# An attention and MLP kernel: denominators of the first four pairs by TensorE, row sums of five pairs partly on GpSimd, a new order of the work

## The chip, the cores and the metric

The kernel runs on one core of a Trainium2 chip. The metric is the device time of the whole program in microseconds; the three runs of the kernel before took 1008.99, 1009.32 and 1010.76 us, with a median of 1009.32 us.

TensorE (PE in the profile) multiplies matrices, VectorE (DVE) does element work and reductions, ScalarE (ACT) activations and copies, GpSimd (POOL) element work between SBUF tiles, SyncE (SP) starts transfers.

## The reference

```python
# attention: q, k, v are (8, 8, 576, 64); omega is (128, 64)
def phi(x):                                   # x is q or k, scaled by 64 ** -0.25
    proj = einsum('bhsd,md->bhsm', x, omega)
    sq = sum(x * x, axis=-1, keepdims=True) / 2.0
    h = proj - sq
    h = h - max(h, axis=-1, keepdims=True)
    return exp(h) / sqrt(m)
q_p, k_p = phi(q_s), phi(k_s)
kv = einsum('bhsm,bhsd->bhmd', k_p, v)
z = sum(k_p, axis=2)
num = einsum('bhsm,bhmd->bhsd', q_p, kv)
den = einsum('bhsm,bhm->bhs', q_p, z) + 1e-06
attn = num / den
# MLP on the 4608 tokens of 512 features, 2048 hidden
h = x @ w_in
out = (h / (1 + exp(-h))) @ w_out
```

The weights arrive in double precision.

## The kernel before

**Tiling.** Attention is cut into 32 pairs: one pair is two heads of one batch, and four pairs (0 to 3) make the first tile of 512 tokens by 512 features. A pair has nine blocks of 128 token rows. For k and for q of each pair the kernel loads the array twice: turned (`raw`, for the projections, L541 and L547) and as it is (`nat`, for the row sums of squares). ACT squares `nat` (`square`, L524), DVE sums its rows (`square_sum`, L533) and takes the maxima of the projections out of PSUM (`top`, L554 and L556); two small reductions (`shift`, L562) make the bias `nb`, and ACT does the exponentials (`expo`, L579).

**Denominator and numerator.** For the first pairs `zsum_direct` (L628, L630) sums k's features over all tokens by multiplying with a block of ones: the result is z, the same in all 128 rows. `denom` (L639) then makes the products of q's features with z and their sums on DVE, ten instructions with an accumulator read behind each, and one reciprocal of 128x9 (L644). `normal` (L669) multiplies q's features by it on GpSimd, three instructions per pair. TensorE turns the normalised features (`turn`, L675), ACT copies them to SBUF (`en_copy`, L685), and `numer` (L711) multiplies them with kv. ACT rounds the result (`x_high`, L730), DVE subtracts to keep the rest (`x_low`, L735); both parts feed the MLP's first product (`stage1`, L886).

**MLP.** For the first three tiles `stage1` and `stage2` (L1132) run over 16 blocks of hidden features. The step for one block needs all four pairs of the tile. Before it, each weight block is put together from double words on DVE (`word`, L809, L811, L815) and split in two on GpSimd (L828, L832). The rest of the tiles go through a scheme with fewer products (L971, L1085), which the change leaves as it is.

**What sets the order.** Every piece of work is a unit with an engine, a cost, a key and its dependences. `Plan.run` lists the units once, on the host, into one order for each engine, by keys that the long string `SHIFTS` moves and by constants such as `STAY` and `JOIN`. On the chip each engine works through its list in order. Where the list leaves TensorE waiting, `pulses` (L500) puts products of a block of ones there, whose results nobody uses.

Of the kernel before, what the change touches and what calls it, by code (L numbers as in the profile page):

```python
# [9 lines left out]
F32 = mybir.dt.float32  # L10
# [4 lines left out]
ALU = mybir.AluOpType  # L15
# [27 lines left out]
LEAD = 4  # L43
WARM = 7
# [10 lines left out]
for _f in range(16):  # L55
# [24 lines left out]
STAY = 5.387  # L80
HANDOFF = {"PE": 0.053, "ACT": 0.034, "DVE": 0.034, "POOL": 0.075, "SP": 0.08}
CALM = 0.341
JOIN = 0.929
WAIT_PE = 0.279
WAIT_ACT = 0.228
WAIT_DVE = 0.243
WAIT_POOL = 0.0
HASTE = 2.036
# [3 lines left out]
EASE = 0.082  # L92
# [11 lines left out]
    "nb": (0.29, 0.37), "ssum": (0.66, 0.745), "den": (3.41, 3.49),  # L104
# [15 lines left out]
    "mkVzphES3T8Pha5xQn+L-UyFew72pi5OPWk0reil7VtnJIflaampwvp00rwVNdu0MlbFQ3mXIpFWXVQqTVWAh2n5lGMadWEFuMErPdltG3I-qz"  # L120
    "Njj8aLV-cUZEz92d39AIqdihAIAIfIA9w9AIA-+20PI88lPhg1dZAyrHN6CW-4JYJLhIAIm2YbHATZSbP1FlHzrMAIxbqCh6AeNPYGeEDRZFsK"
    "V260v0dWO17cdxwGIh6FFERZ7SVN8-6Y+ErCUPAIur-QGICPkQ3mTLqTgNn8yB455fx-u11n3A1DsOJatjjs09nPLXPmgj-4AIC2mdVWPZh82-"
    "xjzpvQAIvTynbmnYgSb8YhfaHoRB4R65pj6NcQmkjEKCYxVofLgLq1btU4iNXeYUbbXSJFJgWWTlLFaBSxmGFLebN1OuZIEtDlEoa0R6i-7i8X"
    "3hOpGSMDyZpXM2Tt2ybo2CJVdtsitDXRPPBkGPTrRwHVFvwHAIXXwOR4F3y+UOXAYYzBCySXA8JyWgRRRcG18vHmCFsmEaF6nJZphVkR6lzX-4"
    "NKBJG-eBVcLHUuEoOBldPSBWtZzb0g7eQKEPHZ6HLceiwdsoG-POE8yii5DsH3AIi4AIAIAIbuJqV+kQAuREAqDOOgAeLKbgknqhwCvE+IQzhg"
    "QOAwZFpr4WUm4Hg0aGD8FNti6bi6VFH2IGqIBHoaVEjfNNOh6+eqbJ1V0x+y-B8x0Tic5hQoMac2zg1AU7ODIYwaZWAIDXXm3hj6mvuUh6spNS"
    "pWcNUNLINoKMH2PyAIoB5TmFKvKzLZLQmZ6HVZ3oEekZAIVReEz17ryW6Mbok-b5LnPNrhg1YcRsjX0UeId1CSAIvxn4vpiAUDFvO0BFAIC+B0"
    "FrFbTvUEECApKUuSksWBUrCHlOJ0FR4dPNUzKgPYPHCfoc44rkr3rYtAP-4rXPDiOMMNLMMSaSAIMTgZEUAuFSNZL8UuSVPVG3AIBSWsE-fjVh"
    "BLA4B+UdAIr-+sR6EaYvI9vtY8APCsFFlNAIdWcsGVG-QnFjLDKYAMAIAISWU-F8kTZHJBCbAoBYZmAMAIASjIwU4xpv21AIAOkWdvQxIWC-r+"
    "mgHBGdytuN-3u2eyDdd5k1zrkcW-DD3qeEc0tElRgu4Gk1zWCyAINfAIs+dc0haFbJAeVF-4JQAI4FpQfP13979ut0A6RbRnZC1Vlye5qjFGf9"  # L130
    "AI8YzTcrjAAILGdf+6VRSKvcidj+knAIfq7erfv62f4uAsnO5ANEbyURoXRHOtRfUiq1BZGGmw9zei4+3L0hzY8diOuwwEcZiMmIB4Dq0ccHqj"
    "ss1b5wwcFV8dnUj2mooJCjAIbQYw42tdhH-4wU7MzYp1e5Z4xVwj6jdf7Wm1lA7l11dICcv7-4zT4D8ju2S3bPd+l7mDVTGqeoiNJq-45K3C7T"
    "FBAIElVBZG4FbZVFmongYIIr5w-48p5M-4-4yyx+AgJok5R47nL1-4AIsb-4efBt9-uV-4m48vvzXGBrNGjykkiQSkeImwQemccx6h-JIBAIDx"
    "BAsjRQPQzqA30by+Dvgrt9-4jsfBgCgUNKGUCow0nsRzn6iX5qO5c81AHeIRy-VPmd-4Cwl2qXuUQigIcVZQ3FabtQAIccGmAIAVqz-47rAITa"
    "bSyXyp3oiNLxWWLfeRp45c5O+L9AnBahluAjNPWhWj92TJ4OCbSElVAIDLYVLEQG4ec0eHnpgjJWD+AJJGZgWgSgF4RLWPD5ZTc1n9jqApAeAI"
    "S5HZAIFLFGFV1JBoWPridVw3w4iddKSCG0HGKQLjd8l6-etrFJ5HBuAI2AvQAIwCDdOEMSlsAIGusDD-KfAuHoE-IKzjJHUZXRLgEjAIGaE6He"
# [54 lines left out]
)  # L191
HOT = 100.0
PULSE = 0.24
IDLE = 0.791
PAD = 0.288
EARLY = 0.9

# [1533 lines left out]
```

## Time and profile before

| what | value |
|---|---|
| median of three runs | 1009.32 us |
| the profiled execution's own time | 1008.95 us |
| its span | 1007.2 us |
| PE busy in the span | 982.9 us (98%) |
| DVE busy | 758.1 us (75%) |
| ACT busy | 637.4 us (63%) |
| POOL busy | 394.2 us (39%) |
| mean granted TensorE clock | 0.995 |

The span is what the profiler saw from first to last instruction; 1.75 us of the execution lie around it. A busy PE counts everything that it multiplies, the fillers of L500 too.

### The profile page before, as it was taken

The page shows a single profiled execution, that of the slowest core. Times are in us where ns is not written, and L with a number is a line of the kernel's source. Part 1 is how long each engine was busy: PE and PEld are TensorE (multiplying, and loading weights), DVE is VectorE, ACT ScalarE, POOL GpSimd, SP SyncE. Part 2 cuts the span into 40 slices and gives each one's busy share as a digit, 9 for nine tenths or more (in the row PEclk, how much of TensorE's full clock was granted, in tenths as well). Part 3 has the DMA queues.
Part 4 walks back from the last instruction along what each step waited for, and adds up shares of the span by engine and source line. Part 5 has one row for each costly group of instructions (what it writes and reads, how often), then busy time and mean ns, then how long its engine had stood idle before and what let it go on. Part 6 is the DMA issues. An engine that isn't in the chain of part 4 may idle for free.

```text
span 1007.2 us, 17418 instructions
## 1 busy us (share of the span) xinstructions
PE 982.9 (98%) x5790; PEld 784.8 (78%) x5790; DVE 758.1 (75%) x1899; ACT 637.4 (63%) x1239; POOL 394.2 (39%) x495
## 2 busy tenths in 40 slices
PE   8789999999999999999999989999999999999998
PEld 7577777777777777778778768777878777888886
DVE  7997988776677767897667799994649987546953
ACT  7778574656557766658988756667678554334541
POOL 1544564677888777654555321330112010000000
PEclk9999999999999999999999999999999999999999
DMA  9757777777777886749788657876545677656682
GB/s 352 284 181 247 257 238 232 243 245 215 262 240 241 273 284 189 265 137 300 270 289 286 213 180 249 270 245 207 167 159 172 203 263 256 194 190 189 188 277 99
DMA packets 107593, 232.94 MB, mean 231 GB/s; under 512 B 14705, under 2 KB 39409, under 8 KB 107505
## 3 DMA queue, kind: packets, MB, share of 16 engines
q1 hardware_dynamic: 107344, 231.58, 70.0%
q8 instruction: 46, 0.75, 0.3%
q14 instruction: 43, 0.34, 0.1%
q10 hardware_dynamic: 160, 0.26, 0.1%
HBM read 182.52 MB, written 49.28 MB: 230 GB/s over the span
## 4 chain that ended last, share of the span: by engine, by line
PE 78%; DVE 15%; ACT 3%; DMA 2%; issue 1%; SPq 0%; DVEq 0%; ACTq 0%
PE ps_acc L971 17%; PE ps_acc L1132 12%; PE ps_acc L1085 11%; PE ps_h L886 7%; PE ps_fx L886 5%; PE ps_att L541 4%; PE ps_att L651 2%; DVE prod L639 2%; PE ps_att L1085 2%; PE ps_att L711 2%; DVE w L1075 2%; PE ps_fx L971 2%; PE ps_att L971 2%; PE ps_h L971 2%; PE ps_h L1085 2%; PE ps_fx L1085 2%
## 5 line engine op out<-in xcount | busy, mean ns | idle before, releaser
L971 PE MATMUL ps_acc<-w,x 128*128 128x512 f32 x768 | 185.8, 395 | 0.3 <-DVE wraw L1018 0.2
L971 PEld LDWEIGHTS ps_acc<-w,x 128*128 128x128 f32 x768 | 141.9, 188 | 32.7 <-DVE wraw L1018 0.8
L669 POOL TENSOR_TENSOR hq<-hq,rd 128x384 f32<-128x384 f32 x96 | 88.6, 947 | 187.8 <-DVE rd L644 144.2
L1132 PE MATMUL ps_acc<-wo,gh 128*128 128x512 f32 x384 | 123.3, 402 | 0.0
L1085 PE MATMUL ps_acc<-w,x 128*128 128x512 f32 x426 | 108.6, 397 | 0.1
L886 PE MATMUL ps_h<-x,w 128*128 128x512 f32 x360 | 97.2, 403 | 0.6 <-ACT gf L1025 0.3
L1085 PEld LDWEIGHTS ps_acc<-w,x 128*128 128x128 f32 x426 | 79.9, 190 | 18.0 <-DVE w L1075 0.6
L1132 PEld LDWEIGHTS ps_acc<-wo,gh 128*128 128x128 f32 x384 | 68.4, 188 | 14.4
L886 PEld LDWEIGHTS ps_h<-x,w 128*128 128x128 f32 x360 | 64.5, 188 | 15.2 <-ACT gf L1025 1.4
L1132 PE MATMUL ps_acc<-wo,gl 128*128 128x512 f32 x192 | 75.4, 393 | 0.4 <-DVE gl L1029 0.4
L1085 PE MATMUL ps_acc<-gh,x 128*128 128x512 f32 x196 | 70.0, 397 | 0.4 <-DVE gf L1105 0.4
L602 POOL TENSOR_TENSOR t<-hk 128x256 f32<-128x256 f32 x48 | 38.2, 816 | 57.5 <-ACT hk L579 31.4
L1029 DVE TENSOR_TENSOR gl<-gf,gh 128x512 fp32r<-128x512 f32 x48 | 44.4, 931 | 17.3 <-ACT gf L1025 17.1
L886 PE MATMUL ps_fx<-x,w 128*128 128x512 f32 x216 | 56.7, 399 | 0.0
L886 PEld LDWEIGHTS ps_fx<-x,w 128*128 128x128 f32 x216 | 39.4, 188 | 10.1 <-issue 1.1
L639 DVE CUSTOM_DVE_ANT_0 prod<-hq,ps_att 128x128 f32<-128x128 f32 (+1 forms) x140 | 40.1, 287 | 8.1 <-PE ps_att L622 2.5
L1085 PEld LDWEIGHTS ps_acc<-gh,x 128*128 128x128 f32 x196 | 36.8, 188 | 9.2 <-DVE gf L1105 0.8
L524 ACT ACTIVATE nat<-nat 128x576 f32<-128x576 f32 x58 | 40.1, 703 | 4.8 <-DMA nat<-qn 2.8
L1132 PEld LDWEIGHTS ps_acc<-wo,gl 128*128 128x128 f32 x192 | 36.0, 188 | 9.0 <-DVE gl L1029 1.0
L685 ACT COPY en<-ps_att 128x384 f32<-128x384 f32 x55 | 25.7, 480 | 22.5 <-PE ps_att L675 18.0
L608 POOL TENSOR_TENSOR t<-t,hk 64x128 f32<-64x128 f32 x48 | 25.0, 520 | 34.6 <-ACT hk L579 31.9
L1085 PE MATMUL ps_acc<-gl,x 128*128 128x512 f32 x98 | 38.3, 391 | 0.0
(464 smaller groups left out, 2461.4 us busy)
## 6 DMA issues: line engine op xcount, KB each, us to landing
x<-ws SPq DMA_DIRECT2D x84, 512.0 KB, 4.2
x<-wt SPq DMA_DIRECT2D x44, 512.0 KB, 4.0
wo<-wo_d SPq DMA_DIRECT2D x32, 512.0 KB, 4.8
x<-wo_d SPq DMA_DIRECT2D x64, 256.0 KB, 3.3
rawk<-kT SPq DMA_DIRECT2D x30, 352.0 KB, 3.9
rawq<-qT SPq DMA_DIRECT2D x30, 352.0 KB, 4.8
v<-v SPq DMA_DIRECT2D x30, 320.0 KB, 4.6
nat<-kn SPq DMA_DIRECT2D x29, 288.0 KB, 4.5
```

The costliest lines, as they stand in the source:

```text
L524: nc.scalar.activation(nat, nat, AF.Square, scale=SCALE * 0.5**0.5)
L541: nc.tensor.matmul(ps[:, i * M : (i + 1) * M], raw[r, o : o + P], oms[r], start=True, stop=True)
L602: nc.gpsimd.tensor_tensor(t[:, step], e[:, 5 * step : 5 * step + 2], e[:, 5 * step + 2 : 5 * step + 4], ALU.add)
L608: nc.gpsimd.tensor_tensor(es[r, j], es[r, j], e[r, MID], ALU.add)
L639: nc.vector.tensor_tensor_reduce(out=prod[r], in0=e[r, c], in1=z[r, j * M : (j + 1) * M], scale=1.0, scalar=GUARD, op0=ALU.mult, op1=ALU.a ...
L669: nc.gpsimd.tensor_tensor(e[:, c], e[:, c], rd[:, c].unsqueeze(2).broadcast_to([P, 3, M]), ALU.mult)
L685: nc.scalar.copy(T["en", n][:, 3 * g * P : 3 * (g + 1) * P], T.pop(("t", n, g)))
L886: nc.tensor.matmul(ph, w[:, i], x[:, j], start=k == 0 and n == 0, stop=k == NK - 1 and n == 2)
L971: nc.tensor.matmul(ph, ws[:, u, kk * P : (kk + 1) * P], o[:, x], start=i in (0, 1, 4) and kk == 0 and n == 0, stop=kk == 1 and n == 2, ski ...
L1029: nc.vector.tensor_tensor(gl, T.pop(("gf", t, f)), T["gh", t, f].bitcast(F32), ALU.subtract)
L1085: nc.tensor.matmul(T["qb", p, chain][d], w[:, u, d * P : (d + 1) * P], x, start=i in (0, 1, 4) and s == 0 and n == 0, stop=s == NS - 1 and ...
L1132: nc.tensor.matmul(T["po", t][j], g[:, js], w, start=f == 0 and n == 0, stop=f == NF - 1 and n == 2)
```

## The change

For pairs 0 to 3 (`n < SHARE`) the sum z is made with a block of ones 64 columns wide, so that it comes out with its 128 features on the partitions, repeated in 64 columns for each head (`zsum_wide`). ACT copies it to SBUF (`z_copy`). q's features are turned without having been normalised, and the numerator's product is followed by the same product with z (`numer_denom`): the denominators stand in 64 rows per head, beside the numerators. ACT copies them out and adds the guard (`den_copy`), DVE inverts them, 128x512 and 128x64, and multiplies them into the numerator (`divide`). `denom` and `normal` are gone for these pairs; `x_high` and `x_low` read the quotient from SBUF.

For pairs 1 to 5 (`TREE`) the squares are made on GpSimd, which then adds the upper half of each row to the lower three times (`fold`: 32, 16, 8 columns). DVE sums the 8 that are left and scales the sums.

`SHIFTS`, and constants of the planner, are new; so the order of the units is new everywhere. The core of the diff:

```diff
+SHARE = 4
+TREE = range(1, 6)
-STAY = 5.387
+STAY = 13.011
-JOIN = 0.929
+JOIN = 2.248
-IDLE = 0.791
-PAD = 0.288
+IDLE = 0.638
+PAD = 0.475
...
     def square(n, who):
         nat = T["nat", n, who]
+        if n in TREE:
+            nc.gpsimd.tensor_tensor(nat, nat, nat, ALU.mult)
+            return
         nc.scalar.activation(nat, nat, AF.Square, scale=SCALE * 0.5**0.5)
...
+        s, nat = sums_at(n, who)[:, 1, :NC], T.pop(("nat", n, who))
+        if n in TREE:
+            nc.vector.tensor_reduce(s, nat[:, :, :8], AX.X, ALU.add, negate=True)
+            nc.vector.tensor_scalar(s, s, SCALE * SCALE * 0.5, None, ALU.mult)
+            return
+        nc.vector.tensor_reduce(s, nat, AX.X, ALU.add, negate=True)
+
+    def fold(n, who, w):
+        nat = T["nat", n, who]
+        nc.gpsimd.tensor_tensor(nat[:, :, :w], nat[:, :, :w], nat[:, :, w : 2 * w], ALU.add)
...
+    def zsum_wide(n, ps):
+        e = T["h", n, "k"]
+        for j in range(2):
+            for i in range(5):
+                c, one = (5 * j + i, ones[:, :D]) if i < 4 else (MID, sides_of[:, j, :D])
+                nc.tensor.matmul(ps[:, j * D : (j + 1) * D], e[:, c], one, start=i == 0, stop=i == 4)
+        T["z", n] = ps
+
+    def z_copy(n):
+        T["zw", n] = zw = new("zw", [P, P])
+        nc.scalar.copy(zw, T.pop(("z", n))[:, :P])
+
+    def numer_denom(n, a, b, c):
+        numer(n, a, b)
+        for ps, lo, hi, at in ((c, 0, MAIN, 0), (b, MAIN, S, P + REST)):
+            for j in range(2):
+                nc.tensor.matmul(
+                    ps[j * D : (j + 1) * D, at : at + hi - lo], T["zw", n][:, j * D : (j + 1) * D],
+                    T["en", n][:, j * S + lo : j * S + hi], start=True, stop=True,
+                )
+        T["dp", n] = [(c, MAIN, 0), (b, REST, P + REST)]
+
+    def den_copy(n):
+        T["dn", n] = new("gl", [P, MAIN]), new("xr", [P, REST])
+        for d, (ps, w, at) in zip(T["dn", n], T["dp", n]):
+            nc.scalar.activation(d, ps[:, at : at + w], AF.Identity, bias=guard)
+
+    def divide(n):
+        T["xf", n], T["xr", n] = new("gf", [P, MAIN]), new("xr", [P, REST])
+        for x, d, (ps, lo, hi, at) in zip((T["xf", n], T["xr", n]), T.pop(("dn", n)), T["num", n]):
+            nc.vector.reciprocal(d, d)
+            nc.vector.tensor_tensor(x, ps[:, at : at + hi - lo], d, ALU.mult)
```

Where it moves instructions, on DVE first: the place behind the exponentials of pair 0. `smk`, `smq` are the sums and maxima, `nbk`, `nbq` the biases, `w_...` in a TENSOR_REDUCE a squared array, `x_391` the first quarter of x. Before:

```order
L639 ISA prod,den<-hq,ps_fx 128x128
L639 ISA den 128x1
L644 RECIPROCAL rd<-den 128x9
L556 TENSOR_REDUCE smq<-ps_acc 128x4 x2
L554 TENSOR_REDUCE smq<-ps_acc 128x1
L562 TENSOR_REDUCE smq<-smq 128x9
L562 TENSOR_REDUCE nbq<-smq 128x9
```

After:

```order
L553 TENSOR_REDUCE smk<-w_194 128x9
L554 TENSOR_SCALAR smk<-smk 128x9
L589 TENSOR_REDUCE smk<-smk 128x9
L589 TENSOR_REDUCE nbk<-smk 128x9
L553 TENSOR_REDUCE smk<-w_199 128x9
L554 TENSOR_SCALAR smk<-smk 128x9
L553 TENSOR_REDUCE smq<-w_197 128x9
L554 TENSOR_SCALAR smq<-smq 128x9
L690 RECIPROCAL gl<-gl 128x512
L691 TENSOR_TENSOR gf<-ps_fx,gl 128x512
L690 RECIPROCAL xr<-xr 128x64
L691 TENSOR_TENSOR xr<-ps_att,xr 128x64
```

The two instructions shown of the 20 rows of `denom` are gone; in their place stand two inversions and two products, and ahead of them three row sums of GpSimd's arrays (194 and 197 of pair 1, 199 of pair 2).

On POOL, from the start of its work. Before, the first rows are pair 0's normalisation and the first weight:

```order
L488 MEMSET sides 64x128 x2
L669 TENSOR_TENSOR hq<-hq,rd 128x384 x3
L828 CAST w_492<-w_468 128x512
L832 TENSOR_TENSOR w_492<-w_468,w_492 128x512
L669 TENSOR_TENSOR hq<-hq,rd 128x384 x3
```

After, three squares and nine halvings come first:

```order
L541 TENSOR_TENSOR w_194<-w_194 128x576
L541 TENSOR_TENSOR w_197<-w_197 128x576
L541 TENSOR_TENSOR w_199<-w_199 128x576
L560 TENSOR_TENSOR w_194<-w_194 128x9x32
L560 TENSOR_TENSOR w_194<-w_194 128x9x16
L560 TENSOR_TENSOR w_194<-w_194 128x9x8
L560 TENSOR_TENSOR w_199<-w_199 128x9x32
L560 TENSOR_TENSOR w_199<-w_199 128x9x16
L560 TENSOR_TENSOR w_199<-w_199 128x9x8
L560 TENSOR_TENSOR w_197<-w_197 128x9x32
L560 TENSOR_TENSOR w_197<-w_197 128x9x16
L560 TENSOR_TENSOR w_197<-w_197 128x9x8
```

Pair 0's and pair 1's normalisations are gone from here, and all ten squares and 30 halvings stand before the third weight's first row.

On PE, the end of pair 0's work. Before, from its turned blocks to its numerator:

```order
L675 MATMUL ps_fx<-ident,hq 128x128 x3
L675 MATMUL ps_acc<-ident,hq 128x128 x3
L675 MATMUL ps_fx<-ident,hq 128x128 x3
L547 MATMUL ps_fx<-oms,w_213 128x128
L711 MATMUL ps_acc<-en,kw 64x512 x2
L711 MATMUL ps_acc<-en,kw 64x64 x2
```

After:

```order
L735 MATMUL ps_acc<-ident,hq 128x128 x3
L719 MATMUL ps_acc<-ident,kt 128x128
L735 MATMUL ps_acc<-ident,hq 128x128 x3
L735 MATMUL ps_fx<-ident,hq 128x128 x3
L771 MATMUL ps_fx<-en,kw 64x512 x2
L771 MATMUL ps_att<-en,kw 64x64 x2
L676 MATMUL ps_att<-en,zw 64x512 x2
L676 MATMUL ps_att<-en,zw 64x64 x2
```

The turns of pair 0 now stand ahead of the other pairs' projections, and the product with z follows the numerator.

## Rows read from the trace of the kernel before

**Rows 1.** The page: busy time by engine; PE in 40 equal slices.

```profile
PE 982.9 (98%) x5790; PEld 784.8 (78%) x5790; DVE 758.1 (75%) x1899; ACT 637.4 (63%) x1239; POOL 394.2 (39%) x495
...
PE   8789999999999999999999989999999999999998
```

**Rows 2.** Stretches: length, busy PE, PEld, DVE, ACT, POOL, clock, DMA share, GB/s.

```profile
0.00:80.00 80.00, 68.32 (x576) 54.99 (x577) 68.01 (x218) 57.85 (x164) 31.07 (x42) 0.96 0.76 270
40.00:50.00 10.00, 7.58 (x69) 5.87 (x65) 9.00 (x37) 7.45 (x26) 4.28 (x5) 0.87 0.80 294
50.00:60.00 10.00, 9.01 (x65) 7.13 (x65) 9.83 (x20) 7.51 (x26) 2.44 (x3) 0.79 0.27 89
80.00:180.00 100.00, 97.62 (x584) 77.10 (x584) 86.95 (x198) 66.51 (x134) 53.53 (x50) 1.00 0.73 246
...
5.73:71.32 65.59, 55.52 (x507) 44.24 (x503) 60.01 (x203) 47.20 (x143) 25.37 (x28) 0.95 0.80 291
```

**Rows 3.** DVE in order of time: start, length, instruction, idle before it.

```profile
5.73 0.75 DVE L533 TENSOR_REDUCE smk<-nat 128x9 f32<-128x576 f32 x1 [4.45 <-ACT nat L524]
...
14.96 0.28 DVE L639 CUSTOM_DVE_ANT_0 prod<-hq,ps_fx 128x128 f32<-128x128 f32 x1
...
18.69 1.23 DVE L556 TENSOR_REDUCE smq<-ps_acc 128x4 f32<-128x512 f32 x2
...
30.14 0.74 DVE L533 TENSOR_REDUCE smq<-w 128x9 f32<-128x576 f32 x1
30.80 0.74 DVE L533 TENSOR_REDUCE smq<-nat 128x9 f32<-128x576 f32 x1
...
60.97 0.28 DVE L639 CUSTOM_DVE_ANT_0 prod<-hq,ps_fx 128x128 f32<-128x128 f32 x1
...
65.03 0.69 DVE L533 TENSOR_REDUCE smq<-nat 128x9 f32<-128x576 f32 x1
...
71.32 0.68 DVE L735 TENSOR_TENSOR x<-ps_att,x 128x512 fp32r<-128x512 f32 x1
```

**Rows 4.** PE in order of time, up to the first second-stage product.

```profile
27.95 2.05 PE L500 MATMUL ps_h<-ones 128*128 128x128 f32 x16 [1.55 <-ACT kw L664]
...
35.54 1.08 PE L711 MATMUL ps_att<-en,kw 128*64 128x512 f32 x4 [1.00 <-ACT en L685]
...
36.66 0.49 PE L547 MATMUL ps_acc<-oms,w 128*128 128x128 f32 x2
36.99 0.39 PE L628 MATMUL ps_acc<-hk,sides 128*128 128x128 f32 x2
...
39.31 1.31 PE L651 MATMUL ps_fx<-hk,w 128*64 128x128 f32 x20
...
80.65 0.62 PE L1132 MATMUL ps_acc<-wo,gh 128*128 128x512 f32 x2
```

**Rows 5.** DVE by group and shape: count, busy us, mean ns, idle before.

```profile
L644 DVE RECIPROCAL rd<-den 128x9 f32<-128x9 f32 x32 | 6.9, 216 | 1.6
...
L554 DVE TENSOR_REDUCE smk<-ps_att 128x1 f32<-128x128 f32 x18 | 5.2, 287 | 7.7 <-ACT en L685 4.4 <-PE ps_att L547 2.0 <-PE ps_att L675 1.2
...
L584 DVE TENSOR_SCALAR hk<-ps_att,nbk 128x128 f32<-128x128 f32 x11 | 3.9, 350 | 0.5 <-ACT en L685 0.2
...
L562 DVE TENSOR_REDUCE smk<-smk 128x9 f32<-128x18 f32 x4 | 0.7, 174 | 0.1
```

**Rows 6.** GpSimd in order of time: pair 0's normalisation.

```profile
18.96 2.40 POOL L669 TENSOR_TENSOR hq<-hq,rd 128x384 f32<-128x384 f32 x3 [17.04 <-DVE rd L644]
```

**Rows 7.** GpSimd's additions on tile t: count, ns least/median/most, first and last start.

```profile
L602 POOL TENSOR_TENSOR t<-hk x48: 722/738/1235, 187.6 to 758.6; 128x256 f32<-128x256 f32 x48
L608 POOL TENSOR_TENSOR t<-t,hk x48: 446/456/1013, 192.5 to 777.9; 64x128 f32<-64x128 f32 x48
```

**Rows 8.** ACT in order of time: squares of pair 1 and 2.

```profile
12.81 1.35 ACT L524 ACTIVATE w<-w 128x576 f32<-128x576 f32 x2
```

**Rows 9.** DVE's first or-step of a weight, 0 to 130 us: least/median/most.

```profile
L811 DVE SCALAR_TENSOR_TENSOR w<-wre,w x20: 680/693/1775, 22.8 to 128.1; 128x512 uint32<-128x512 uint32 x20
```

More of the change, by code (lines that the diff above doesn't have):

```diff
@@ L120 @@
[L120 to L124, printed above, removed]
@@ L1178, in attention_mlp @@
                 order=before, alloc=[(HOMES.get(("nat",) + w, "nat"), ("nat",) + w)], lat=1.1)
[L1179 removed]
+            folded = n in TREE
+            add(("sq",) + w, "POOL" if folded else "ACT", 0.7, at(n, 2 * i - 4, 13 + 10 * i - 32), lambda n=n, who=who: square(n, who),
                 after=[("nat",) + w], alloc=[(f"sm{who}", ("sm",) + w)])
+            for x in (32, 16, 8) if folded else ():
+                add(("fold", n, who, x), "POOL", 0.4, at(n, 2 * i - 4 + 0.02 * (32 - x), 13 + 10 * i - 32), lambda n=n, who=who, x=x: fold(n, who, x),
+                    after=[("sq",) + w if x == 32 else ("fold", n, who, 2 * x)])
             add(("ssum",) + w, "DVE", 0.76, at(n, 2 * i - 3, 14 + 10 * i - 32), lambda n=n, who=who: square_sum(n, who),
[L1182 removed]
+                after=[("fold", n, who, 8) if folded else ("sq",) + w], order=prev("ssum"), free=[("nat",) + w])
             o = 6.2 + 10.8 * i
@@ L1264, in attention_mlp @@
             alloc=[("kw", ("kw", n))], free=[bk(kx)], reads=[bk(kx)])
-        add(("den", n), "DVE", 3.5, at(n, 8, 34.2), lambda n=n: denom(n), after=e["q"] + [zn],
-            order=[("den", n - 1)] if n else [], alloc=[("den", ("den", n)), ("rd", ("rd", n))], free=[bk(zn)], reads=[bk(zn)])
-        plan.freed_by[("den", n)] = [("den", n)]
+        shared = n < SHARE
+        if shared:
+            add(("zc", n), "ACT", 0.3, at(n, 6.9, 0), lambda n=n: z_copy(n), after=[zn], alloc=[("zw", ("zw", n))], free=[bk(zn)])
+        else:
+            add(("den", n), "DVE", 3.5, at(n, 8, 34.2), lambda n=n: denom(n), after=e["q"] + [zn],
+                order=[("den", n - 1)] if n > SHARE else [], alloc=[("den", ("den", n)), ("rd", ("rd", n))], free=[bk(zn)], reads=[bk(zn)])
+            plan.freed_by[("den", n)] = [("den", n)]
         for g in range(3):
-            add(("norm", n, g), "POOL", 0.85, at(n, 9 + 0.1 * g, 37 + 0.1 * g), lambda n=n, g=g: normal(n, g),
-                after=[("den", n)], order=[("norm", n, g - 1)] if g else [], free=[("rd", n)])
+            if not shared:
+                add(("norm", n, g), "POOL", 0.85, at(n, 9 + 0.1 * g, 37 + 0.1 * g), lambda n=n, g=g: normal(n, g),
+                    after=[("den", n)], order=[("norm", n, g - 1)] if g else [], free=[("rd", n)])
             joint = DIRECT <= n < NWIN - 1
@@ L1294, in attention_mlp @@
         homes_of = [(f"x{k}{t % 2}", ("x", t, k))] if t < PLAIN else []
-        add(nm, "PE", dur, at(n, 10, 60.5), lambda a, b, n=n, f=kv_numer if follow else numer: f(n, a, b),
-            after=after, alloc=homes_of, free=free, banks=2)
+        if shared:
+            add(nm, "PE", 2.2, at(n, 10, 60.5), lambda a, b, c, n=n: numer_denom(n, a, b, c), after=after + [("zc", n)], alloc=homes_of,
+                free=free + [("zw", n)], banks=3)
+            add(("dn", n), "ACT", 0.8, at(n, 10.1, 0), lambda n=n: den_copy(n), after=[nm], alloc=[("gl", ("dn", n)), ("xr", ("dr", n))], free=[bk(nm, 2)])
+            add(("dv", n), "DVE", 0.9, at(n, 10.15, 0), lambda n=n: divide(n), after=[("dn", n)], alloc=[("gf", ("xf", n)), ("xr", ("xr", n))],
+                free=[bk(nm, 0), bk(nm, 1), ("dn", n), ("dr", n)])
+        else:
+            add(nm, "PE", dur, at(n, 10, 60.5), lambda a, b, n=n, f=kv_numer if follow else numer: f(n, a, b),
+                after=after, alloc=homes_of, free=free, banks=2)
         p, j = divmod(t - PLAIN, 2)
```

201 lines of the change are left out of this document (111 added, 90 removed), and 2 rows, old and new, of the table RINGS.

## Prediction

> **What bounds the kernel now.** First the page: PE is busy for 982.9 of 1007.2 us, and its slices are full but for the first three, the one with an 8 near 600 us and the last [rows 1]. So outside the start time is only won by taking work from PE, and the change takes none there. [...] Part of the busy time is filler: 16 rows for eight products take 2.05 us, so the 16 products in the order cost 16 x 0.26 = 4.2 us [rows 4]. **The start thus holds 11.7 + 2.9 + 4.2 = 18.8 us that are no work**; from 80 to 180 us it is 2.4 us [rows 2].
>
> Who makes PE wait there? DVE. From its first row sum at 5.73 us to the subtraction that finishes the first tile's x, at 71.32, it works through its list almost without a gap: 60.0 of 65.6 us are busy, and what is missing is the few hundredths between one short instruction and the next [rows 2, 3]. PE has 55.5 busy us in the same stretch, ACT 47.2, POOL 25.4. Behind that subtraction lie the products for three hidden blocks, and the first second-stage product starts at 80.65 [rows 4]. From then on PE is saturated. So the change is to be priced by what it does to DVE's list up to the fourth subtraction; PE's own work is a second floor.
>
> **DVE's list.** Removed: four denominators. The first occupies DVE from 14.96 to 18.69, the fourth from 60.97 to 65.03 [rows 3]: 3.73 and 4.06 us, four at 3.9 are 15.6. (Pair 4's denominator stands ahead of the fourth subtraction before and after.) The ten row sums of pairs 1 to 5 cost 0.66 from start to start [rows 3]; the new one reduces 72 elements, near the 0.17 of the row with 18 inputs, and a scaling that waits for it [rows 5]; I take 0.35. Ten save 3.1.
>
> Added, four times: an inversion and a product of 512 columns, and both of 64. The products are like the two maxima that take 1.23 together [rows 3]: 0.6, and 0.15 for the small one. The inversion of 512 is not in the trace; the nearest row is the one of nine elements at 0.216 us [rows 5]. A reduction of 18 inputs to 9 takes 0.174, so 0.042 us are in excess. If that is a fixed charge, 512 elements stream like everything else, in 0.6 us. If it belongs to the elements, each costs (0.042 + 0.009)/9 = 5.7 ns more than in a streaming pass, and the two inversions 3.5 + 0.5 = 4.0 us instead of 0.75. A row speaks for the fixed charge: an element-wise instruction on 128 elements takes 0.350 where a reduction over as many takes 0.287 [rows 5], an excess of 0.063 that cannot depend on nine elements. I take 0.75, so 1.5 us for a pair, 6.0 for four; the upper end, 4.75 a pair, is a rival below.
>
> In sum DVE's list gets 15.6 + 3.1 - 6.0 = **12.7 us shorter**. Two things take some of it back.
>
> **GpSimd.** It loses 4 x 2.40 us of normalising [rows 6] and gets ten squares and 30 halvings. By the normalisation (384 elements in 0.80) a square of 576 costs 1.2 and the three halvings, 504 elements, 1.05; by the additions on t (256 elements in 0.738, 128 in 0.456, so 0.17 + 2.2 ns an element) 1.44 and 1.63 [rows 6, 7]. One array thus costs 2.25 to 3.1 us, ten cost 22 to 31. POOL was busy for 25 of DVE's 65.6 us [rows 2], so there is room; the order is what hurts. Ahead of pair 0's first inversion DVE waits for three arrays, whose twelve GpSimd instructions take 6.8 to 9.2 us and can begin when the arrays are in, about 11.5 (ACT has all three squared from 12.81 on [rows 8]). They end between 18 and 21. DVE's own work up to there, two row sums, six maxima of 0.6 and small ones, is some 7.5 us from 5.73, so it stands idle for 5 to 7 us; I take 5.5. Queued behind that wait are pair 0's inversion and the maxima of pair 1's q. Pair 0's own chain would not be much sooner: exponentials, turns, copies, products and one copy end at about 18 too.
>
> [...] The or-step that reads two SBUF tiles has a least time of 0.68 and a worst of 1.775 [rows 9], and some 16 steps with two SBUF inputs stand in the new list up to there (the weights' or-steps, x's subtractions); with GpSimd half as busy again I put 2 us more on them. [...]
>
> So the fourth subtraction comes at 71.32 - 12.7 + 5.5 + 2 = 66.1, 5.2 us earlier, and the first second-stage product, 9.3 us behind it as before, at 75.4.
>
> **PE's floor.** Ahead of that product both orders hold the same 12 projections, 45 turned blocks and 36 first-stage products; after has, in addition, pair 4's kv and numerator (1.3 + 1.1 us [rows 4]), which need not be done later: 2.4 us. The four new products with z cost as much as the numerator, 35.54 to 36.66 [rows 4]: 4 x 1.1 = 4.5. The sum z took 2.3 us (36.99 to 39.31); with half the columns it lies between that and the 1.31 of kv; I take 1.7, which saves 2.4 in four. Nineteen fillers stand in the new order, 4.9 us. Work before was 80.65 - 18.8 = 61.9; now 61.9 + 2.4 + 4.5 - 2.4 + 4.9 = 71.3. That leaves 4.1 us of idle up to 75.4: DVE still sets the end, with PE close behind.
>
> **The sum.** 5.2 us earlier plus 2.4 us done ahead are 7.6. Against that: at the first second-stage product the new DVE list has seven weights put together where the old had eight to nine, and each weight costs DVE two or-steps of 0.69 [rows 9] and a shift, in a stretch where it is busy for 87 of 100 us [rows 2]. I put 1.2 us more idle there. Past 180 us the number of changes between kinds of product on PE is the same in both orders (153), so I take nothing. **6.4 us off the profiled 1008.95 is 1002.5; off the median 1009.32, which lies 0.4 above it, it is 1002.9.** ACT loses ten squares and gains four copies of 0.6, four small ones: it had 18 us of air in the stretch and hides both. The SP queue has the same loads in another order; the fourth pair's arrays are in well before they are needed.
>
> **Rivals.**
>
> *The inversion costs by the element.* Place: the first row of `divide` on DVE, four times, with the maxima of the next pairs queued behind it. At 4.0 us instead of 0.75 the four pairs cost 13 us more on the list that sets the end, and 1002.9 becomes 1016; with some of it in gaps 1013 to 1016. It decides from about 4 ns an element, where the 6.4 us are gone. For it: the excess of 0.042 us in the only row [rows 5]. Against it: the element-wise row with the same excess. [...]
>
> [...]
>
> *The change does what it says, but PE is not waiting for DVE.* Then the 2.1 us of added PE work and three more fillers would show at once: 1012. The idle PE beside the busy DVE [rows 2] speaks against it; I count it with the first rival's chance.
>
> **How the numbers follow.** The forecast, 1002.9, has 0.50 (999 to 1006.5, from 3 to 6.5 us of waits and 1.3 to 2.3 for z); the first rival 0.34 (1009 to 1018, most near 1015); the waits 0.16 (1005.5 to 1009). To hold 8 in 10 the range needs the forecast, the waits and half of the first rival: **999 to 1015**; the forecast's own is 999 to 1006.5. About 0.2%, 2 us, is what a measurement can tell from no change. Faster by more: 0.48 of the forecast, 0.09 of the waits, 0.02 of the rival, 0.59. Within: 0.11. Slower: 0.30, nearly all of it the first rival.
>
> **What would show it.** The inversion of 128x512 at 0.6 to 0.7 us (right) or above 2 (the first rival). The fourth subtraction at 63 to 68 us, the first second-stage product at 73 to 78, with DVE idle for about 5 us before pair 0's inversion, waiting for GpSimd. PE idle in the first 75 us at 4 to 6. From 80 to 180 us idle of 3 to 4, and nothing changed past it. The forecast is wrong if a second stretch appears in which PE waits, or if the new order leaves PE idle past 180 us where its slices are full now.

## The result, and the profile after

The changed kernel takes 1024.24 us (median of 4 runs, 1018.78 to 1026.26), the kernel before 1010.04 beside it: a ratio of 1.0133, 95% interval 1.0091 to 1.0175. Run a second time it gave 1021.56 and a ratio of 1.0119 [1.0092, 1.0145]. It is 1.2 to 1.3% slower, and 6.6 to 9.2 us above the upper end of the predicted range. The profiled execution is its fastest: 1018.78 us with a span of 1017.0, against 1008.95 and 1007.2 before.

The page (busy time; PE in slices; granted clock) and the stretches, the answers to [rows 1, 2]:

```profile
PE 992.3 (98%) x5828; PEld 794.8 (78%) x5828; DVE 764.1 (75%) x1842; ACT 631.8 (62%) x1233; POOL 412.6 (41%) x523
...
PE   8898999999999999999999999999999999999998
...
PEclk9898999999999999999999999999999999999999
```

```profile
0.00:80.00 80.00, 68.43 (x567) 55.74 (x567) 62.13 (x141) 47.99 (x150) 43.64 (x63) 0.91 0.65 224
20.00:30.00 10.00, 7.72 (x71) 6.94 (x70) 9.65 (x15) 3.40 (x11) 9.53 (x12) 0.86 1.04 399
30.00:40.00 10.00, 10.00 (x73) 7.95 (x73) 9.20 (x18) 8.82 (x27) 6.93 (x12) 0.80 0.41 121
40.00:50.00 10.00, 5.87 (x48) 5.06 (x49) 9.60 (x22) 5.30 (x19) 5.75 (x7) 0.88 0.48 163
50.00:60.00 10.00, 10.00 (x87) 8.96 (x88) 6.40 (x18) 6.42 (x24) 4.45 (x6) 0.78 0.31 93
80.00:90.00 10.00, 7.57 (x49) 6.01 (x51) 8.58 (x17) 5.99 (x11) 2.76 (x4) 0.66 0.89 304
80.00:180.00 100.00, 97.07 (x584) 77.90 (x585) 89.89 (x200) 67.58 (x137) 53.98 (x51) 0.97 0.75 251
...
96.18:1017.00 920.82, 910.12 (x5184) 728.26 (x5182) 687.92 (x1676) 571.94 (x1062) 365.40 (x456) 1.00 0.70 229
```

PE is as busy in the first 80 us as before (68.4 and 68.3), but the granted clock is 0.91 where it was 0.96. The stretch at 40 to 60 us is as before (0.88 and 0.78); new are the one at 20 to 40 us (0.86 and 0.80, before 1.00) and the one at 80 to 90 us (0.66, before 1.00), which runs mostly at half the full clock (0.50 from 82 to 88 us). Behind the first second-stage product (the last row; it starts at 96.18, before at 80.65) 920.8 us are left, before 926.6. So 15.5 us are lost up to there and 5.7 come back behind it: PE is busy there for 910.1 us instead of 913.9, since pair 4's products are done ahead as the prediction said (it had put 2.4), and idle for 10.7 us instead of 12.7. That makes 9.8 us, the difference of the two spans. Of the 15.5 only 2.3 are more idle time of PE (14.0 us up to the product, before 11.7). An estimate by the prediction's own way of reckoning, busy time times the missing share of the clock in the five stretches above, puts 8.6 us on the clock where it had 2.9 (7.58 x 0.13 + 9.01 x 0.21 [rows 2]): 5.7 us more. The rest, some 7.5 us, is work that now stands ahead of that product.

VectorE in order of time, the answer to [rows 3] (start, length, instruction, the idle time before it): pair 0's first short row sum and its division, then the division of the fourth pair and its x subtraction.

```profile
16.49 0.23 DVE L553 TENSOR_REDUCE smk<-w 128x9 f32<-128x72 f32 x1 [3.82 <-POOL w L560]
16.75 0.48 DVE L554 TENSOR_SCALAR smk<-smk 128x9 f32<-128x9 f32 x1
...
20.97 3.34 DVE L690 RECIPROCAL gl<-gl 128x512 f32<-128x512 f32 x1
...
27.01 1.45 DVE L799 TENSOR_TENSOR x<-gf,x 128x512 fp32r<-128x512 f32 x1
...
78.22 3.29 DVE L690 RECIPROCAL gl<-gl 128x512 f32<-128x512 f32 x1
81.62 0.69 DVE L691 TENSOR_TENSOR gf<-ps_att,gl 128x512 f32<-128x512 f32 x1
82.22 0.54 DVE L690 RECIPROCAL xr<-xr 128x64 f32<-128x64 f32 x1
82.86 0.23 DVE L691 TENSOR_TENSOR xr<-ps_att,xr 128x64 f32<-128x64 f32 x1
...
84.24 0.68 DVE L799 TENSOR_TENSOR x<-gf,x 128x512 fp32r<-128x512 f32 x1
```

An inversion of 512 columns takes 3.3 us, nearly five times the product behind it (0.69). The fourth subtraction stands at 84.24 instead of 71.32. The groups over the first 100 us show that no inversion is an exception:

```profile
L690 DVE RECIPROCAL gl<-gl 128x512 f32<-128x512 f32 x4 | 13.3, 3330 | 0.0
...
L690 DVE RECIPROCAL xr<-xr 128x64 f32<-128x64 f32 x4 | 2.2, 544 | 0.0
L554 DVE TENSOR_SCALAR smq<-smq 128x9 f32<-128x9 f32 x5 | 2.2, 430 | 0.2
```

And PE, up to the first second-stage product, waits most for the products behind the inversions (L691; waits by releaser: sum, times, longest):

```profile
PE ps_acc L568 <- DVE gf L691: 3.3, 2, 1.9
PE ps_att L568 <- DVE gf L691: 2.5, 1, 2.5
PE ps_att L574 <- DVE xr L691: 2.3, 1, 2.3
PE ps_att L574 <- ACT hk L606: 2.2, 1, 2.2
```

The projections of the next pairs write the PSUM tiles (`ps_acc`, `ps_att`) that the division's products read: 8.1 us of waits. In the kernel before PE's longest wait for VectorE there is 0.7 us, its first instruction apart. Behind one of these waits the trace shows a loss of its own. PE in order of time, behind the 2.3 us for pair 0's division:

```profile
25.95 0.49 PE L574 MATMUL ps_att<-oms,rawq 128*128 128x128 f32 x2 [2.28 <-DVE xr L691]
26.28 1.00 PE L665 MATMUL ps_fx<-ones,hk 128*128 128x64 f32 x8
...
27.49 1.92 PE L665 MATMUL ps_fx<-ones,hk 128*128 128x64 f32 x8
```

The same eight rows take 1.00 us and, 1.2 us later, 1.92: PE waited 2.28 us, and its granted clock, 1.00 from 26 to 27 us, was 0.50 from 28 to 34.

### The profile page after: what moved, and what is told of

Its sections match the earlier page's. It is cut to its first block, busy times and chain, and to the rows that moved or that the text cites. A ratio compares the mean times of both kernels' runs of the same rounds, so it can differ in the third digit from the quotient of the medians.

```text
span 1017.0 us, 17440 instructions
## 1 busy us (share of the span) xinstructions
PE 992.3 (98%) x5828; PEld 794.8 (78%) x5828; DVE 764.1 (75%) x1842; ACT 631.8 (62%) x1233; POOL 412.6 (41%) x523
## 4 chain that ended last, share of the span: by engine, by line
PE 80%; DVE 13%; issue 1%; ACT 1%; DMA 1%; SPq 0%; DVEq 0%; ACTq 0%
PE ps_acc L1035 18%; PE ps_acc L1149 12%; PE ps_acc L1196 12%; PE ps_h L950 7%; PE ps_fx L950 5%; PE ps_att L568 4%; PE ps_att L1149 3%; DVE omr L699 2%; PE ps_att L1035 2%; PE ps_att L771 2%; PE ps_h L1149 2%; PE ps_att L711 2%; PE ps_h L1035 1%; PE ps_att L735 1%; DVE w L844 1%
## 5 line engine op out<-in xcount | busy, mean ns | idle before, releaser
L1035 PE MATMUL ps_acc<-w,x 128*128 128x512 f32 x810 | 196.3, 396 | 1.3 <-DVE w L844 0.7
L1035 PEld LDWEIGHTS ps_acc<-w,x 128*128 128x128 f32 x810 | 149.5, 188 | 35.6 <-DVE wraw L1082 1.3
L729 POOL TENSOR_TENSOR hq<-hq,rd 128x384 f32<-128x384 f32 x84 | 78.9, 963 | 202.3 <-DVE rd L704 172.8
L1149 PE MATMUL ps_acc<-w,x 128*128 128x512 f32 x426 | 108.0, 395 | 0.4 <-DVE w L1139 0.4
L1149 PEld LDWEIGHTS ps_acc<-w,x 128*128 128x128 f32 x426 | 79.1, 188 | 18.3 <-DVE w L1139 0.9
L950 PE MATMUL ps_h<-x,w 128*128 128x512 f32 x348 | 91.8, 400 | 0.0
L699 DVE CUSTOM_DVE_ANT_0 omr<-hq,ps_att 128x128 f32<-128x128 f32 (+1 forms) x180 | 51.6, 286 | 16.8 <-PE ps_att L649 10.8
L950 PE MATMUL ps_fx<-x,w 128*128 128x512 f32 x228 | 60.0, 402 | 2.5 <-DVE hk L611 2.5
L1093 DVE TENSOR_TENSOR gl<-gf,gh 128x512 fp32r<-128x512 f32 x48 | 41.8, 875 | 18.6 <-ACT gf L1089 18.5
L950 PEld LDWEIGHTS ps_fx<-x,w 128*128 128x128 f32 x228 | 41.9, 190 | 12.0 <-POOL wo L892 2.7
L543 ACT ACTIVATE nat<-nat 128x576 f32<-128x576 f32 x54 | 37.1, 695 | 5.3 <-DMA nat<-kn 2.8
L745 ACT COPY en<-ps_att 128x384 f32<-128x384 f32 x46 | 21.9, 483 | 25.1 <-PE ps_att L735 20.8
```

The source lines that it names most:

```text
L543: nc.scalar.activation(nat, nat, AF.Square, scale=SCALE * 0.5**0.5)
L699: nc.vector.tensor_tensor_reduce(out=prod[r], in0=e[r, c], in1=z[r, j * M : (j + 1) * M], scale=1.0, scalar=GUARD, op0=ALU.mult, op1=ALU.a ...
L729: nc.gpsimd.tensor_tensor(e[:, c], e[:, c], rd[:, c].unsqueeze(2).broadcast_to([P, 3, M]), ALU.mult)
L745: nc.scalar.copy(T["en", n][:, 3 * g * P : 3 * (g + 1) * P], T.pop(("t", n, g)))
L950: nc.tensor.matmul(ph, w[:, i], x[:, j], start=k == 0 and n == 0, stop=k == NK - 1 and n == 2)
L1035: nc.tensor.matmul(ph, ws[:, u, kk * P : (kk + 1) * P], o[:, x], start=i in (0, 1, 4) and kk == 0 and n == 0, stop=kk == 1 and n == 2, ski ...
```

## Experiments

Theory: the inversion's price is the error of the prediction. Rival: the rest of the new order (its waits for GpSimd, PE's fixed order) is slow by itself. Ratios are to the kernel before on the same chip. Unless said otherwise an experiment keeps the changed kernel's order and edits only what is issued.

**The changed kernel again.**

> The changed kernel once more, unaltered. Its profiled execution took 1018.78 us, its three timed ones 1023.1 to 1026.3 at a lower mean granted clock (0.983 beside 0.990). If the profiled one was only lucky, this profile comes at 1023 to 1026 and shows the stretch where a second 5 us of the clock go; I expect that in the first 100 us, where the clock of the first profile was already 0.90. If the two figures belong to how the executions are taken, the profile is again near 1019 and the timed ones near 1024.

1021.56 us (1019.26 to 1024.97), the profiled one again the fastest: 1019.26, clock 0.990. The second reading held in the main: the profile is again near 1019, and the others, 1020.9 to 1025.0, reach up to the 1024 that was expected of them. Both profiles agree within 0.5 us at every point that is used here (the fourth subtraction at 84.24 and 84.49, the first second-stage product at 96.18 and 96.39). Where the other executions lose their 1.7 to 7.5 us no profile of this kernel shows; their clock was 0.982 to 0.988.

**No inversion.**

```
-            nc.vector.reciprocal(d, d)
+            nc.vector.tensor_scalar(d, d, 1.0, None, ALU.mult)
```

> The changed kernel in its own order, with each of the eight inversions replaced by a multiplication of the same tile by 1.0: the numerators are multiplied by the denominators and not divided by them. This is the case that the prediction took as likeliest (an inversion that streams). Theory (the inversion's 3.33 and 0.54 us a pair are the whole error): DVE's list gets 4 x (3.87 - 0.6) = 13 us shorter, the fourth subtraction comes at 68 to 72 instead of 84.2, the first second-stage product at 79 to 83, the profiled time at 1004 to 1008, the median near the forecast of 1002.9 to 1008. Rival (the new order's waits for GpSimd and its fixed order cost as much by themselves): not below 1012.

1010.50 us, ratio 1.0010 [0.9998, 1.0022]: 11.1 us less than the changed kernel in the same comparison. The stand-ins took 0.48 and 0.76 us instead of 3.33 and 0.54:

```profile
L690 DVE TENSOR_SCALAR xr<-xr 128x64 f32<-128x64 f32 x4 | 3.0, 762 | 0.0
...
L690 DVE TENSOR_SCALAR gl<-gl 128x512 f32<-128x512 f32 x4 | 1.9, 479 | 0.0
```

So VectorE's list lost 4 x 2.63 = 10.5 us, and the end came sooner by about as much. That is not a chain of VectorE alone: the fourth subtraction came 8.4 us sooner (75.82 for 84.24), and 2 us more were won behind it, where the clock from 80 to 90 us is 1.00 instead of 0.66. The inversions are worth these 11 us. But the time lies between the two expectations, above the theory's and below the rival's, and 7.6 us are still missing to the forecast of 1002.9. In its trace (VectorE and PE in order of time; this profile's first row sum came 1.5 us later than the changed kernel's, behind a load):

```profile
52.39 0.69 DVE L583 TENSOR_REDUCE smq<-ps_att 128x4 f32<-128x512 f32 x1 [4.01 <-PE ps_att L568]
...
75.82 0.68 DVE L799 TENSOR_TENSOR x<-gf,x 128x512 fp32r<-128x512 f32 x1
```

```profile
42.44 0.80 PE L574 MATMUL ps_att<-oms,w 128*128 128x128 f32 x2 [2.33 <-ACT hk L606]
...
85.79 0.62 PE L1196 MATMUL ps_acc<-wo,gh 128*128 128x512 f32 x2
```

Now PE is late too: it waits 2.33 us for exponentials, runs at a clock of 0.62 from 40 to 50 us, and VectorE waits 4.0 us for a projection. The subtraction is at 75.8 where the forecast had 66.1.

**Two pairs without inversion.** The same edit for n < 2 (stream_01) and for n > 1 (stream_23).

> The changed kernel in its own order, with the inversions of pairs 0 and 1 alone replaced by a multiplication by 1.0 (their numerators are multiplied by the denominators and not divided); pairs 2 and 3 are inverted. All four replaced gave 1010.5, none 1021.6 to 1024.2. If each inversion costs the same at the end (VectorE's list is one chain from the start to the fourth subtraction), this gives 1016 to 1018. If the first two fall into time in which VectorE waits for something else anyway, it gives 1020 to 1023.

> The counterpart: pairs 2 and 3 have the multiplication by 1.0 and are not divided, pairs 0 and 1 are inverted. One chain: 1016 to 1018, as its counterpart. If only the last two stand on the path that sets the end: 1011 to 1013.

1016.84 us, ratio 1.0071 [1.0055, 1.0088], and 1014.81, ratio 1.0048 [1.0032, 1.0064]. The first is as one chain would have it; the second lies between its two expectations. Against the changed kernel's 1.0119 the first two pairs give back 4.8 us and the last two 7.2; all four gave 11.0. The parts add up (12.0 and 11.0, within the intervals), for 5.3 us of VectorE's time each. So the first two inversions don't lie in time that is free anyway. Whether the last two weigh more than the first can't be told: the intervals of 4.8 and 7.2 us overlap.

**The squares and row sums back.** In `square`, `square_sum` and `fold` (the short sum and its scaling in `square_sum` go too):

```
     def square(n, who):
...
-            nc.gpsimd.tensor_tensor(nat, nat, nat, ALU.mult)
-            return
...
     def fold(n, who, w):
-        nc.gpsimd.tensor_tensor(nat[:, :, :w], nat[:, :, :w], nat[:, :, w : 2 * w], ALU.add)
+        pass
```

> The changed kernel in its own order, with the squares of pairs 1 to 5 back on ScalarE at the same places, no halvings, and the full row sums on VectorE; the inversions stay. Theory (the inversion is the error, the halvings are right): DVE gains ten times 0.745 - 0.61 us = 1.4 us of work, and loses the 3.8 us wait for GpSimd ahead of pair 0's inversion in part (ScalarE has the squares by 13 to 14 us); ScalarE gets 7 us more. In sum within 4 us of the changed kernel, 1015 to 1023 profiled. [...]

1024.27 us, ratio 1.0138 [1.0118, 1.0158], as the changed kernel: the squares on GpSimd and the waits for them are not what makes it slow, though the profiled execution, 1025.05, lies 2 us above the theory's range. Its trace shows where the time went that VectorE no longer waits for GpSimd:

```profile
21.71 3.35 DVE L687 RECIPROCAL gl<-gl 128x512 f32<-128x512 f32 x1 [4.56 <-ACT gl L682]
```

Without GpSimd VectorE waits for ScalarE's copy of pair 0's denominators, which stands behind the squares there, and the first inversion begins at 21.71 us instead of 20.97. With GpSimd the copy, behind pair 1's exponentials on ScalarE, ended at 20.70, so pair 0's own chain was about as late as the row sums. The same edit without the inversions:

> The changed kernel in its own order with both edits: no inversion (a multiplication by 1.0 in its place, so the numerators are multiplied by the denominators), and the squares and the full row sums of pairs 1 to 5 back on ScalarE and VectorE. With the squares on GpSimd this was 1010.5, so 8 us of the forecast of 1002.9 are missing without any inversion. If GpSimd's work is where they went (its scalings of 9 elements took up to 0.83 us where free ones take 0.17), this is faster than 1010.5: 1004 to 1008. [...]

1008.97 us, ratio 1.0001 [0.9989, 1.0014], beside 1.0010 with GpSimd's squares: above the 1004 to 1008 of the expectation, and the intervals of the two overlap. **In this order the second part of the change neither gains nor costs anything that can be measured**; by the intervals at most some 2.6 of the missing 7.6 us are GpSimd's.

**The second part alone**, in the order of before: the squares of pairs 1 to 5 and their halvings issued on GpSimd where the squares stood on ScalarE, the short sums on VectorE.

```
+        if n in range(1, 6):
+            nc.gpsimd.tensor_tensor(nat, nat, nat, ALU.mult)
+            for w in (32, 16, 8):
+                nc.gpsimd.tensor_tensor(nat[:, :, :w], nat[:, :, :w], nat[:, :, w : 2 * w], ALU.add)
+            return
```

> The kernel before, in its own order, with the second part alone: the squares of pairs 1 to 5 and their three halvings on GpSimd, issued where the squares stood on ScalarE, and the short row sums on VectorE. The denominators are those of before. Theory (the halvings do what the prediction said: ten row sums save 0.3 us each of VectorE's list; GpSimd's instructions wait behind its normalisations, which stand in its queue in another order than would suit them): between 1005 and 1013, near the kernel before. Rival (VectorE's instructions with two inputs in SBUF and its short scalings are held up by GpSimd's for longer than the row sums save): 1012 to 1020.

1023.30 us, ratio 1.0131 [1.0113, 1.0148]: above both expectations. PE's waits in its first 90 us; the last line is the first one's counterpart in the kernel before:

```profile
PE ps_acc L685 <- POOL hq L679: 6.6, 6, 3.0
PE ps_h L896 <- DVE x L745: 4.9, 2, 3.9
...
PE ps_acc L675 <- POOL hq L669: 3.4, 6, 1.1
```

GpSimd is busy for 52.8 of the first 80 us (31.1 before), and pairs 0 to 3 are still normalised there (hq): PE's turned blocks stand behind the halvings. What the rival names is there as well: the scalings of nine elements take up to 0.96 us (0.17 where they are shortest), and PE waits 4.9 us for VectorE's x subtraction. So in the order of before the second part costs 13 us, with the normalising still on GpSimd; whether an order made for it alone would do better was not tried.

**VectorE's list lighter still.** No inversion and nothing in its place, squares on ScalarE, and the row sums of pairs 1 to 5 over 8 of 64 columns:

```
-            nc.vector.reciprocal(d, d)
...
+        if n in TREE:
+            nat = nat[:, :, :8]
         nc.vector.tensor_reduce(s, nat, AX.X, ALU.add, negate=True)
```

> The changed kernel in its own order with VectorE's list made lighter still: no inversion and nothing in its place (the numerators are multiplied by the denominators), the squares on ScalarE, and the row sums of pairs 1 to 5 taken over 8 of the 64 columns only, without halvings and scalings (the sums are wrong). Against the kernel with squares on ScalarE and a multiplication for each inversion (1009.0) VectorE loses 4 x 1.0 us of multiplications and ten times 0.745 - 0.22 us, 9 us in all. Theory (VectorE's list still sets the end of the start, and the missing 8 us of the forecast are terms of that list that I took too low): 1000 to 1004. Rival (with the inversion gone the start is set by TensorE and by what it waits for, the floor that the prediction put 4 us lower): 1006 to 1010.

1005.27 us, ratio 0.9950 [0.9935, 0.9966]: 5.1 us less (0.9950 to 1.0001) for 4 x 1.26 us of stand-ins and ten times 0.52 us of row sums, 10.3 us of VectorE's list; it lies just above the first expectation, below the second. The two profiles differ by less, 3.6 us of span and 2.6 at the first second-stage product (83.76 and 81.19). The first 80 us, then the stretch from 40 to 50 us in the kernel with the stand-ins (squares on ScalarE) and in this one, and what PE still waits for in the 80 us:

```profile
0.00:80.00 80.00, 72.06 (x640) 57.96 (x641) 52.48 (x146) 62.62 (x180) 17.36 (x26) 0.98 0.77 270
...
40.00:50.00 10.00, 7.67 (x48) 7.03 (x50) 7.33 (x19) 7.95 (x28) 2.01 (x2) 0.68 0.53 176
40.00:50.00 10.00, 7.98 (x88) 7.17 (x88) 7.34 (x21) 9.53 (x34) 2.08 (x3) 1.00 0.59 212
```

```profile
PE ps_att L565 <- ACT hk L603: 1.1, 1, 1.1
PE ps_att L512 <- DVE guard L504: 1.1, 1, 1.1
PE ps_h L516 <- ACT hq L603: 1.1, 1, 1.1
PE ps_acc L715 <- ACT kt L712: 0.9, 1, 0.9
```

VectorE is busy for 52 of 80 us, and but for the first instruction PE's waits of over half a microsecond are all for ScalarE. The first second-stage product starts at 81.19, still not ahead of the 80.65 of before; what this kernel wins over the one before lies behind it (922.3 us instead of 926.6). Part of the gain is the clock's, 1.00 from 40 to 50 us instead of 0.68. And the squares are on ScalarE here, which is busy for 62.6 of 80 us (53.0 with the squares on GpSimd and no inversion), so its waits may be this edit's own. That 81 us are the floor of the new order on PE is therefore not shown, only that PE hardly waits for VectorE any more.

**The inversion on ScalarE**, as the exponential of the negative logarithm.

```
-            nc.scalar.activation(d, ps[:, at : at + w], AF.Identity, bias=guard)
+            nc.scalar.activation(d, ps[:, at : at + w], AF.Ln, bias=guard)
+        for d in T["dn", n]:
+            nc.scalar.activation(d, d, AF.Exp, scale=-1.0)
...
-            nc.vector.reciprocal(d, d)
```

> The changed kernel in its own order, with the inversion moved to ScalarE: the logarithm in place of the copy, then the exponential of its negative, both with a table load ahead (1.28 us each in the profile), and VectorE only multiplies. VectorE loses 4 x 3.87 us; ScalarE, busy for 41.5 of 65.6 us, gains four times 2 x 1.28 + 0.7 + 0.35, about 14.5 us. Theory (VectorE's list sets the end, and ScalarE has the room): the fourth subtraction at 70 to 74, 1003 to 1008. Rival (the turned blocks' copies and the exponentials queue behind the table loads and PE waits for them): 1010 to 1018.

1015.28 us, ratio 1.0051 [1.0033, 1.0069]: 6.3 us faster than the changed kernel, not faster than before. Groups on ScalarE (first 100 us), and VectorE's largest wait (first 90 us):

```profile
L685 ACT ACT_TABLE_LOAD x4 | 5.1, 1283 | 0.1
L687 ACT ACT_TABLE_LOAD x4 | 5.1, 1283 | 0.1
```

```profile
DVE gf L692 <- ACT gl L687: 11.7, 4, 5.0
```

VectorE waits 11.7 us for the four inversions, and PE's three longest waits there, 2.5, 2.4 and 2.1 us, are for ScalarE's copies: the rival's range and its path, with the pair's own chain beside the queue of copies.

**The inversion on GpSimd**, as a power.

```
+    minus = const.tile([P, 1], F32, tag="minus", name="minus")
+    nc.vector.memset(minus, -1.0)
...
-            nc.vector.reciprocal(d, d)
+            nc.gpsimd.tensor_tensor(d, d, minus[:, :1].broadcast_to([P, hi - lo]), ALU.pow)
```

> The changed kernel in its own order with the inversions on GpSimd, as a power of -1, in place of VectorE; the rest as it is. No run shows the price of a power on GpSimd. GpSimd was busy for 36.7 of 65.6 us. If it costs an element what a multiplication there does (1.12 us for 576 elements), it gives what ScalarE's version without the table loads would, 1006 to 1012, since the pair's own chain keeps its length less 3 us; if it costs several times that, GpSimd's halvings of the next pairs queue behind it, and it gives 1020 to 1060.

1374.98 us, ratio 1.3610 [1.3584, 1.3637]. The groups on GpSimd:

```profile
L692 POOL TENSOR_TENSOR gl<-gl,minus 128x512 f32<-128x512 f32 x4 | 328.1, 82022 | 9.3 <-ACT gl L687 9.3
L692 POOL TENSOR_TENSOR xr<-xr,minus 128x64 f32<-128x64 f32 x4 | 42.1, 10520 | 0.0
```

A power took 160 to 164 ns an element; worse than the far end of the expectation.

**An order made for the true price.** The planner's cost of the division, and the shifts of the due times searched again:

```
-    ... "dv": (1.46, 1.54), ...
+    ... "dv": (5.3, 5.4), ...
```

> The changed kernel with the same work, in an order made anew: the planner's cost of the division step is 5.3 us in place of 1.46 (the trace: 3.33 + 0.69 + 0.54 + 0.23 us and the gaps), and the numbers that shift the units' due times were searched again for it, though far shorter than those of the two kernels, so that past the start the order is worse and only the start is to be compared. If the wrong price in the plan was at fault (the order put work behind an inversion that it took for short), the fourth subtraction comes near 76 to 80 us, where it stands without any inversion, and the first second-stage product at 84 to 89, instead of 84.2 and 96.2. If the inversions are the fault whatever the order, both come within 3 us of the changed kernel's. The whole time I expect at 1020 to 1035 either way.

1037.98 us, ratio 1.0275 [1.0257, 1.0293], 3 us above what was expected of the whole. The fourth subtraction is at 83.94 us, as in the changed kernel; the first second-stage product at 91.58, 4.6 us sooner, which fits neither expectation. So the subtraction speaks for the inversions whatever the order, the product perhaps for some fault of the plan as well. With a search this short it can't be settled whether a good order exists at this price; that stays open.

## Why the prediction was wrong, point by point

**The step that failed: the price of the inversion.** The prediction held two rows against each other, the 0.042 us by which nine inverted elements exceed a reduction, and the 0.063 by which an element-wise instruction on 128 does [rows 5], and took the excess for a fixed charge. It belongs to the elements. Three sizes now lie on a line: 0.216 us for 9, 0.544 for 64, 3.330 for 512, that is 6.0 ns an element between the first two and 6.2 between the last two. The upper end that was worked out for the rival was 4.75 us a pair; measured are 3.33 + 0.69 + 0.54 + 0.23 = 4.79. So the bound was right, and the choice between the bounds was not. The row chosen as a likeness differed from the inversion in its operation and in where it read (PSUM, the inversion SBUF); a small row that is over its likeness can't say whether the excess is fixed, because a fixed charge and a charge by nine elements look alike in it. The trace's 3.33 lies near the 3.5 of that bound and far from the 0.6 taken. No run shows the 1018 at which the prediction let the rival's span end; its own sum from the rows ends at 1016.

Its worth at the end is shown: 11.1 us when all four give way to a multiplication, 4.8 and 7.2 for the halves. The rival's 13 us more and its 1016 were a little high in the first and, by the median, 6 to 8 us low in the second, because the forecast under it was too low as well.

**The second error: what is late next.** Without any inversion the kernel takes 1010.5, 7.6 us above the forecast. Three terms of VectorE's list were low. The short sum with its scaling was put at 0.35 and took 0.22 + 0.41; in the changed kernel's trace the scaling of nine elements takes 0.17 where GpSimd is idle (at 45.67, 46.01 and 58.34 us) and 0.22 to 0.83 beside it. The stand-ins took 1.24 a pair where 0.75 was put, the two products 0.92 where 0.75 was. Together 2.8 + 2.0 + 0.7 = 5.5 of the 9.7 us by which the subtraction is late in this trace (75.8 for 66.1). The rest is not shown term by term; the 4.0 us in which VectorE waits for PE's projection are nearly as long. The prediction's work of 71.3 us up to the first second-stage product (its 18.8 us that are no work are 80.00 - 68.32 = 11.7 of idle, the 2.9 of the clock and 4.2 of filler [rows 2, 4]) was about right (in the lightest kernel 73.2 busy us there at a mean clock of 0.98), but it left only 4.1 us of idle. The lightest kernel still has 7.9, in waits for ScalarE and in the first 20 us, and stream has 9.9 and a stretch at a clock of 0.62 (40 to 50 us). So from about one to one (the inversions) the end's answer to VectorE's list falls to half or less (5.1 us by the ratios, 3.6 by the profiles, for 10.3): the forecast took 12.7 us off one engine's list and followed the end down past the point at which another engine sets it. The waits, to which the prediction gave 0.16 and 1005.5 to 1009, show in the kernel without inversions, though that, at 1010.5, lies above this span.

**A term that wasn't there.** Half the columns in z were to save 0.6 us a pair. PE in order of time, without the inversion:

```profile
24.23 1.00 PE L665 MATMUL ps_fx<-ones,hk 128*128 128x64 f32 x8
25.07 0.39 PE L665 MATMUL ps_fx<-sides,hk 128*128 128x64 f32 x2
25.29 1.06 PE L665 MATMUL ps_fx<-ones,hk 128*128 128x64 f32 x8
26.18 0.39 PE L665 MATMUL ps_fx<-sides,hk 128*128 128x64 f32 x2
26.41 0.89 PE L516 MATMUL ps_acc<-ones 128*128 128x128 f32 x6
```

From 24.23 to 26.41 are 2.18 us, against 2.32 [rows 4]: a product of 64 columns goes out hardly faster here than one of 128, and the saving is 0.14 us a pair.

**What held.** VectorE waits 3.8 + 0.6 + 1.0 = 5.4 us for GpSimd ahead of pair 0's division (5.5 were put), and the twelve GpSimd instructions ahead of it take 8.5 us, from 11.4 to 19.9 (6.8 to 9.2 were put). But little of this wait was a price of GpSimd's: pair 0's own chain, put at 18, ended at 20.7, and with the squares on ScalarE VectorE waits 2.0 + 4.6 us there instead. Pair 4's products are done ahead. The x subtraction, whose two inputs now lie in SBUF, took 1.45 and 1.48 us beside GpSimd's squares and 0.68 where GpSimd did not work; these two make 1.6 of the 2 us put on VectorE's steps with two SBUF inputs. That sum was the author's estimate; how GpSimd's work lengthens them no run shows, and an or-step at 32.85 us took 0.69 beside its halvings. That the removed denominators and row sums stand on the path is not shown by a run of its own; it fits with the inversions, put in the denominators' place, standing there. "Nothing changed past 180 us" holds too: PE is idle there for 10.2 us, before for 10.3. The 2.0 us of idle that PE no longer has behind the first second-stage product lie before that, 0.5 us up to 180 where there were 2.4; the prediction had put 1.2 us more there.

## What to carry to other kernels

An operation of a kind that the trace has only at a few elements has no price at 512: where the bounds lie five times apart and the sign hangs on it, the forecast is the bound that decides, or none. The number of elements is part of the design here: `denom` inverted 128x9 for a pair, `divide` inverts 128x576, every denominator 64 times, and 0.22 us became 3.87. Taking work off the engine that sets the end is worth about its length only until the next engine's own list and waits take over; that floor is to be summed with the idle time that it has had so far, not with the least that could remain. In the changed kernel PE ran at a clock of 0.50 for 6 us (28 to 34 us) shortly behind its 2.28 us of wait for the division, so a wait may cost more than its own length. And a part of a change can depend on the other: in the order of before, with the squares and the normalising both on GpSimd (busy for 52.8 of the first 80 us), PE waits 6.6 us for it, 3.4 without the squares.

## What the runs showed of the hardware

- VectorE's inversion took 0.216 us for 128x9, 0.544 for 128x64 and 3.330 for 128x512, 6.2 ns for each further element of a partition between the last two, and its length did not change beside a busy GpSimd (3.34 us at 20.97, and 3.35 with the squares on ScalarE, where GpSimd is idle from 10 to 30 us).
- GpSimd's power took 160 to 164 ns an element (82.0 us for 128x512, 10.5 for 128x64).
- A scaling of nine elements on VectorE took 0.17 us with GpSimd idle (changed kernel, 45.67 us) and up to 0.83 with GpSimd at work (20.22 us).
- On TensorE five fp32 products of 64 columns (ten rows of the trace) took 1.09 us, five of 128 columns 1.16, both at a granted clock of 1.00.
